# Pair 0 takes the raw first layer, four pairs take the cosine by a quarter turn, and the order is written anew

## The chip, the cores and the metric

The kernel runs on one core of a Trainium2 chip. A core has five engines that each work through their own instructions in program order: PE (matrix multiply, with PEld for its weight loads), DVE (vector), ACT (activation functions), POOL (general), and SP, which here only issues transfers. Sixteen DMA engines move the data. The metric is the device time of one execution in microseconds (us). Before the change it is 197.97 us, the median of 5 runs from 197.55 to 199.03.

## The reference

Two steps in a row. The first is a gated recurrence for 4 batches, 8 heads, 768 tokens and 48 channels per head. Every channel has a complex gate whose magnitude is capped, and a state:

```
scale = minimum(mag, 0.999) / (mag + 1e-06)        # mag = |a_re + i a_im|
new_re = ar*S_re - ai*S_im ;  new_im = ar*S_im + ai*S_re
S_re, S_im = new_re + k v^T, new_im
y[t] = q[t] . S_re
```

The second is a feed-forward block on x, the 384 values per token that the heads give together:

```
xn = (x - mu) / sqrt(var + 1e-06) * g_ln
out = x + maximum(xn @ w_ch1, 0) @ w_ch2           # 384 -> 1536 -> 384
```

## The kernel before

The tokens are cut into 24 chunks of 128; two chunks make a pair, so there are 12 pairs, three per batch. For a pair P the steps are named `step.P...`, and for a chunk n `step.n`. Pair 0 alone does its gate steps in two halves of four heads (`.0.0` and `.0.1`).

The gates go in logarithm and phase. `ln` takes the logarithm of a_re, `iv` its reciprocal, `r` the quotient a_im/a_re, `r2` and `u` the logarithm of 1+r*r, `l` the capped log magnitude (two DVE instructions, L449 and L451), `th` the arctangent of r. PE sums both along the tokens by triangular matrices: `dec` (L459) and `ph` (L474, L477). `e` and `en` are the exponentials of the decay. The phase stands in PSUM as turns scaled so that the low 16 bits of the word are the fraction of a turn; these are read as int16, which wraps the angle. `sin` (L502) reads them directly. For the cosine, `abs` (L496 on ACT or L498 on DVE) writes the absolute value to SBUF and `cos` (L505) takes the sine of a quarter minus it. `car` hands the phase to the next pair.

`ke` and `qe` scale k and q, `ks` and `qs` multiply them by cosine and sine, `kT`, `qT` transpose on PE and `ksT`, `qsT` copy the result out; from pair 3 on many of these are DMA transposes that SP issues (L566). `am` is the score matrix, `atm` masks it, `gm` and `G` carry the state, `y` is the output of a chunk, `x` its copy to SBUF.

For the feed-forward part, `bn` takes mean and variance of x, `xtr` and `xT` transpose x, `mm1.P.g.part` is the first layer in three groups g of two parts (L684, twelve matmuls a group), `relu.P.g` follows, `mm2.n.g` is the second layer (L705, four matmuls a step), and `ot` (L719; or `oa` on ACT and `ot` on POOL) scales by 1/sqrt(var) from `rstd` (POOL, L670 and L672), adds x, and `st` stores. The mean is not taken from x. It is taken out of the weights once: `wgc` builds a matrix of g_ln/384, `wp.g` multiplies w1 by it on PE (L367), and `wc.g.e`, nine DVE instructions (L371), replace w1 by g_ln*w1 minus that product. All first layers, pair 0's too, need `wc`.

w1 and w2 come by two transfers that POOL issues (`wl.0`, L350, and `wl.1`, L352), which also cast them to bf16. Two `gate` steps (L347) hold them back: POOL copies one element of a tile that SP loads, and so waits until it has landed.

The order on every engine is written out by hand in one string, `PLAN`: each word is a step, its engine and its PSUM bank. An engine does its steps in exactly that order; a step that waits holds all that follow it on its engine. `warm` steps are matmuls on constants that only keep PE running. `tab` steps load ACT's function table: logarithm and exponential are in one set, sine and arctangent in another.

Of the kernel before, what the change touches and what calls it, by code (L numbers as in the profile page):

```python
# [26 lines left out]
         "ks": 3, "qs": 3, "ksT": 4, "qsT": 4, "atm": 3, "G": 4, "x": 10, "stats": 4,  # L27
# [6 lines left out]
GATES = (("k", 0, 1), ("aim", 1, 0))  # L34
# [17 lines left out]
warm.60:P4 warm.61:P4 ph.1.0:P2 k.1.1:S qe.0.1.0:V cos.0.1:A qs.0.1.0:V cos.0.0:A dec.0.0:P1 sin.0.0:A0
aim.3.0:S vf.1.1:S k.1.0:S abs.1.0:V2 car.1.0:V2 vf.1.0:S q.1.1:S ks.0.1.0:G pad.qs.1:G mask:G tab.log.1:A
en.0.0:A1 e.0.0:A1 qs.0.1.1:V ke.0.0.0:V qe.0.0.0:V ks.0.0.0:V ks.0.0.1:V warm.62:P5 warm.63:P5 warm.64:P5
warm.65:P5 warm.66:P5 warm.67:P5 warm.68:P5 warm.69:P5 warm.70:P5 warm.71:P5 warm.72:P5 warm.73:P5
warm.74:P5 warm.75:P5 warm.76:P5 warm.77:P5 warm.78:P5 warm.79:P5 warm.80:P5 warm.81:P5 warm.82:P5 kT.1:P4
k.2.0:S wl.0:G qs.0.0.1:V u.1.0:A ln.2.0:A qs.0.0.0:V dps.0:P5 k.2.1:S iv.2.0:A l.1.0:V kT.0:P6 qT.1:P7
tab.trig.1:A cos.1.0:A v.0:A ksT.0:V6 r.2.0:G ksT.1:V4 decc.0:V5 wgc:V qsT.1:V7 qT.0:P0 gm.0:P1 dec.1.0:P4
am.1:P6 th.2.0:A sin.1.0:A2 tab.log.2:A e.1.0:A4 r2.2.0:G u.2.0:A pad.qs.2:G qsT.0:V0 am.0:P2 G.0:V1
atm.1:V6 atm.0:V2 y.1:P0 y.0:P6 ln.3.0:A iv.3.0:A wp.2:P7 qe.1.0.0:G x.0:A6 l.2.0:V dec.2.0:P2 wl.1:G  # L60
en.1.0:A4 wp.0:P6 e.2.0:A2 x.1:A0 wc.2.0:V7 wc.2.2:V7 en.2.0:A2 are.4.0:S xtr.0:P0 wc.2.1:V7 dps.1:P7
xtr.1:P4 r.3.0:G xT.0:A0 wp.1:P5 decc.1:A7 ph.2.0:P2 wc.0.0:V6 wc.0.1:V6 bn.0:V wc.0.2:V6 r2.3.0:A xT.1:A4
wc.1.2:V5 wc.1.1:V5 wc.1.0:V5 ke.1.0.0:G ke.1.0.1:G ks.1.0.0:G v.1:G qe.1.0.1:G mm1.0.2.1:P6 gm.1:P1 G.1:V1
mm1.0.2.0:P6 relu.0.2:V6 u.3.0:A aim.4.0:S ks.1.0.1:V qs.1.0.1:V qs.1.0.0:V bn.1:V rstd.0:G abs.2.0:A2
tab.trig.2:A th.3.0:A cos.2.0:A mm1.0.0.1:P4 mm1.0.1.1:P0 mm1.0.0.0:P4 relu.0.0:V4 sin.2.0:A2 k.3.0:S
q.2.1:S mm1.0.1.0:P0 ph.3.0:P6 l.3.0:V relu.0.1:A0 kT.3:P2 gm.2:P3 vf.2.0:S q.2.0:S k.3.1:S kT.2:P0 qT.2:P1
ksT.2:V0 qsT.2:V1 mm2.0.0:P4 mm2.0.1:P4 mm2.0.2:P4 sin.3.0:A6 am.2:P0 abs.3.0:A6 G.2:A3 ksT.3:A2 ke.2.0.0:G
gm.3:P3 qT.3:P5 ke.2.0.1:V ks.2.0.0:V tab.log.3:A ln.4.0:A iv.4.0:A ks.2.0.1:G r.4.0:G atm.2:V0 mm2.1.0:P2
mm2.1.1:P2 qsT.3:V5 vf.2.1:S aim.6.0:S am.3:P0 mm2.1.2:P2 car.3.0:A6 G.3:V3 q.3.1:S q.4.1:S ot.0:V4 kT.5:P3
atm.3:V0 tab.trig.3:A th.4.0:A qe.2.0.1:G qe.2.0.0:G y.2:P5 q.3.0:S are.6.0:S vf.3.1:S st.0:S y.3:P4 x.2:A5  # L70
x.3:A4 kT.4:P6 xtr.2:P7 ot.1:V2 bn.2:V xT.2:V7 xtr.3:P2 xT.3:V2 ksT.4:V6 dec.3.0:P0 mm1.1.0.1:P4
mm1.1.0.0:P4 r2.4.0:A mm1.1.1.1:P6 qs.2.0.1:V qs.2.0.0:V qT.5:P2 mm1.1.1.0:P6 ksT.5:V3 bn.3:V qT.4:P3
tab.log.4:A en.3.0:A0 v.2:A e.3.0:A0 relu.1.1:A6 ph.4.0:P0 relu.1.0:V4 vf.3.0:S gm.4:P4 ke.3.0.1:G qsT.4:V3
am.4:P6 qsT.5:V2 mm2.2.0:P5 am.5:P2 mm2.2.1:P5 tab.trig.4:A cos.3.0:A G.4:A4 rstd.1:G ke.3.0.0:G qe.3.0.1:G
are.5.0:S aim.5.0:S abs.4.0:V0 sin.4.0:A0 car.4.0:A0 atm.4:V6 mm1.1.2.0:P6 dps.3:P4 mm1.1.2.1:P6 tab.log.5:A
u.4.0:A atm.5:V2 qe.3.0.0:G ks.3.0.1:G ks.3.0.0:V qs.3.0.1:V relu.1.2:V6 qs.3.0.0:V y.5:P0 y.4:P1 l.4.0:V
mm2.3.0:P2 x.5:A0 kT.7:P3 mm2.3.1:P2 x.4:A1 xtr.4:P0 mm2.2.2:P5 xtr.5:P1 ln.5.0:A k.4.0:S iv.5.0:A decc.3:A4
ln.6.0:A q.4.0:S k.5.1:S v.3:G ksT.7:V3 dec.4.0:P6 xT.5:V1 xT.4:A0 mm2.3.2:P2 e.4.0:A6 en.4.0:A6 iv.6.0:A
bn.4:V mm1.2.1.1:P0 ot.2:V5 r.5.0:G qsT.7:S r.6.0:G r2.5.0:V mm1.2.1.0:P0 gm.6:P3 qe.4.0.1:V bn.5:V rstd.2:G
ke.4.0.0:G relu.2.1:A0 u.5.0:A mm1.2.0.1:P4 mm1.2.0.0:P4 tab.trig.5:A th.5.0:A mm1.2.2.1:P6 qe.4.0.0:G  # L80
am.7:P0 mm1.2.2.0:P6 ot.3:V2 qsT.6:S ksT.6:S k.5.0:S vf.4.1:S th.6.0:A relu.2.2:A6 vf.4.0:S st.2:S cos.4.0:A
G.6:V3 k.4.1:S q.5.1:S st.1:S gm.7:P3 dps.4:P2 relu.2.0:V4 mm2.5.0:P4 atm.7:V0 l.5.0:V am.6:P0 atm.6:V0
are.8.0:S y.7:P5 mm2.5.1:P4 q.5.0:S ph.5.0:P6 aim.7.0:S mm2.4.0:P0 y.6:P1 x.7:A5 xtr.7:P5 mm2.5.2:P4
r2.6.0:V bn.7:V ke.4.0.1:G v.4:V x.6:V1 xtr.6:P1 sin.5.0:A6 abs.5.0:A6 xT.7:A5 cos.5.0:A decc.4:A2
mm2.4.1:P0 mm2.4.2:P0 are.7.0:S k.6.1:S G.7:V3 ot.5:V4 tab.log.6:A u.6.0:A xT.6:V1 qs.4.0.0:V mm1.3.0.0:P6
dec.5.0:P4 ks.4.0.1:V mm1.3.1.1:P2 ks.4.0.0:V gm.8:P1 mm1.3.0.1:P6 mm1.3.1.0:P2 qs.4.0.1:V ot.4:V0 e.5.0:A4
qe.5.0.0:G kT.9:P0 en.5.0:A4 relu.3.0:A6 kT.8:P4 st.4:S l.6.0:V ln.8.0:A ksT.8:A4 G.8:A1 bn.6:V st.3:S
k.6.0:S qsT.9:S relu.3.1:V2 qe.5.0.1:V qs.5.0.0:V rstd.3:G q.6.1:S aim.8.0:S st.5:S mm1.3.2.0:P6 qT.8:P5
mm1.3.2.1:P6 ln.7.0:A gm.9:P1 relu.3.2:A6 vf.5.0:S mm2.7.0:P4 dec.6.0:P2 qs.5.0.1:G qsT.8:V5 mm2.7.1:P4
iv.7.0:A G.9:V1 ksT.9:V0 ke.5.0.0:V en.6.0:A2 am.8:P6 e.6.0:A2 r.7.0:V vf.5.1:S ph.6.0:P0 mm2.7.2:P4  # L90
qT.10:P5 am.9:P2 vf.6.1:S r2.7.0:A iv.8.0:A ke.5.0.1:V atm.8:V6 ks.5.0.0:G ks.5.0.1:G u.7.0:A y.8:P6 x.8:A6
tab.trig.6:A sin.6.0:A0 r.8.0:G ke.6.0.0:G qT.11:P7 qsT.10:V5 atm.9:V2 qsT.11:V7 mm2.6.0:P5 mm2.6.1:P5
y.9:P6 abs.6.0:A0 car.6.0:A0 kT.10:P7 bn.8:V x.9:V6 ksT.10:V7 xtr.8:P2 kT.11:P3 xtr.9:P6 mm2.6.2:P5 xT.9:A6
xT.8:V2 ksT.11:V3 am.10:P0 vf.6.0:S th.7.0:A mm1.4.1.0:P6 am.11:P2 th.8.0:A ke.6.0.1:G v.5:G mm1.4.1.1:P6
ot.6:V5 oa.7:A4 k.8.1:S are.9.0:S mm1.4.0.0:P4 mm1.4.0.1:P4 atm.10:V0 gm.10:P0 relu.4.1:A6 l.7.0:V
ks.6.0.1:V ph.7.0:P6 y.10:P1 cos.6.0:A atm.11:V2 G.10:V0 y.11:P0 relu.4.0:A4 mm2.9.0:P2 mm1.4.2.1:P4 x.10:V1
x.11:V0 r2.8.0:A mm1.4.2.0:P4 mm2.8.0:P3 dec.7.0:P0 mm2.8.1:P3 mm2.9.1:P2 ks.6.0.0:G car.7.0:A6 sin.7.0:A6
tab.log.7:A ln.9.0:A q.6.0:S q.8.0:S bn.9:V bn.10:V abs.7.0:A6 e.7.0:A0 qe.6.0.1:G qe.6.0.0:G rstd.4:G
ot.7:G v.6:G relu.4.2:V4 mm2.8.2:P3 xtr.10:P4 bn.11:V qs.6.0.0:V en.7.0:A0 qs.6.0.1:V gm.12:P5 dps.6:P6
# [102 lines left out]
def kernel(  # L202
# [54 lines left out]
    def T(name, i):  # L257
        return tiles[name][i % RINGS[name]]
# [512 lines left out]
```

## Time and profile before

| what | value |
|---|---|
| median of 5 runs | 197.97 us |
| the profiled execution's own time | 198.91 us |
| its span, first to last instruction | 197.0 us |
| PE busy | 176.4 us, of which `warm` (L734) 11.1 |
| DVE / ACT / POOL busy | 160.1 / 164.0 / 107.9 us |
| data moved | 37.76 MB, mean 192 GB/s |

The page shows the busy time of each engine, a strip of the span in 40 slices (digits are tenths busy; the line of the PE clock is what was granted), the DMA queues, the chain of work that ended last, and the costliest groups of instructions. A group's line gives the engine, the operation, output and inputs, the shapes, the count, the busy time with the mean of one in ns, and the idle time of the engine before these instructions with what ended it. Other views list instructions in order of time, or the busy time in chosen stretches.

### The profile page before, as it was taken

Reading aid. Unit: us, or ns where it says so; the run is one execution under the profiler, and the core shown is the slowest. Engines: PE = TensorE matmul, PEld = TensorE weight load, DVE = VectorE, ACT = ScalarE, POOL = GpSimd, SP = SyncE. Lnnn points to the kernel's source line nnn. Section 1 sums busy time; section 2 is a strip of 40 time slices with the busy share of each in tenths; the row PEclk is TensorE's granted clock in tenths of the full one; section 3 lists DMA queues with packets and bytes.
Section 4 is the critical chain, followed back from the end, with each engine's and each line's share of the span. In section 5 each row is a group of like instructions: output and inputs, shape, how many; then the busy total and the mean of one; then the engine's idle time right before and its main releaser. Section 6 shows DMA issues by size and latency. Waiting matters only on the chain.

```text
span 197.0 us, 5115 instructions
## 1 busy us (share of the span) xinstructions
PE 176.4 (90%) x2032; PEld 134.7 (68%) x2032; DVE 160.1 (81%) x268; ACT 164.0 (83%) x226; POOL 107.9 (55%) x127
## 2 busy tenths in 40 slices
PE   4788467989999999899999997999999999997992
PEld 3575443576787777587887785787877768686771
DVE  1359999899999999999998799699969969835702
ACT  4799994999899999999999999997979999464260
POOL 8545558435939268134958699325981376430230
PEclk9999965899999999999999999999999999999999
DMA  5999998999899599899899999999998999994222
GB/s 138 230 235 251 178 238 113 189 218 235 174 254 223 113 173 244 211 242 247 162 206 224 221 147 281 181 209 236 234 199 149 154 212 136 235 194 137 80 83 82
DMA packets 132937, 37.76 MB, mean 192 GB/s; under 512 B 127921, under 2 KB 132529, under 8 KB 132913
## 3 DMA queue, kind: packets, MB, share of 16 engines
q1 hardware_dynamic: 130960, 35.07, 85.6%
q0 software_dynamic: 1952, 2.36, 7.4%
q8 instruction: 16, 0.26, 0.5%
q14 instruction: 9, 0.07, 0.1%
HBM read 28.31 MB, written 4.72 MB: 168 GB/s over the span
## 4 chain that ended last, share of the span: by engine, by line
PE 46%; DVE 22%; ACT 10%; DMA 9%; issue 5%; SPq 3%; POOL 2%; DVEq 0%; POOLq 0%; ACTq 0%
PE banks L705 16%; PE banks L684 13%; DMA qsT<-qs 5%; DVE atm L280 4%; PE banks L584 3%; SPq L566 3%; DVE l L449 3%; PE banks L459 3%; DVE l L451 2%; DVE h L697 2%; PE banks L561 2%; DMA are<-in_a_re_dram 2%; DMA q<-in_q_dram 2%; ACT L739 2%; DVE w1b L371 2%
## 5 line engine op out<-in xcount | busy, mean ns | idle before, releaser
L705 PE MATMUL banks<-w2b,h 128*128 128x384 bf16 x288 | 55.5, 326 | 1.2 <-DVE atm L280 1.1
L684 PE MATMUL banks<-xT,w1b 128*128 128x256 bf16 x432 | 52.4, 272 | 1.0 <-DVE w1b L371 0.5
L684 PEld LDWEIGHTS <-w1b 128*128 128x128 bf16 x432 | 41.3, 98 | 7.9 <-issue 2.0
L705 PEld LDWEIGHTS <-h 128*128 128x128 bf16 x288 | 26.2, 97 | 14.9 <-issue 1.6
L280 DVE TENSOR_TENSOR atm<-banks,mask 128x1024 bf16<-128x1024 f32 x24 | 28.8, 1216 | 4.3 <-PE banks L584 4.2
L695 ACT ACTIVATE h<-banks 128x1024 bf16<-128x1024 f32 x27 | 27.0, 1022 | 6.3 <-PE banks L684 6.2
L739 ACT ACT_TABLE_LOAD x20 | 25.7, 1283 | 1.1 <-PEq L755 0.8
L280 POOL TENSOR_TENSOR ks<-ke,trig 128x768 bf16<-128x768 bf16 (+1 forms) x11 | 17.9, 1635 | 12.0 <-DVE ke L280 7.4
L280 POOL TENSOR_TENSOR qe<-q,e 128x384 bf16<-128x384 f32 x16 | 15.8, 996 | 13.2 <-ACT e L463 9.7
L280 POOL TENSOR_TENSOR r<-aim,are 128x768 f16<-128x768 f32 (+1 forms) x9 | 16.7, 1851 | 10.8 <-ACT are L433 10.8
L280 POOL TENSOR_TENSOR ke<-k,en 128x384 bf16<-128x384 f32 x17 | 17.1, 1014 | 8.8 <-ACT en L463 8.1
L719 DVE SCALAR_TENSOR_TENSOR ot<-banks,rstd,x 128x384 f32<-128x384 f32 x20 | 12.0, 609 | 8.8 <-PE banks L705 6.0
L584 PE MATMUL banks<-qsT,ksT 128*128 128x128 bf16 x192 | 15.3, 227 | 2.9 <-DVE qsT L277 1.6
L584 PEld LDWEIGHTS <-ksT 128*128 128x128 bf16 x192 | 13.0, 102 | 5.3 <-issue 3.7
L734 PE MATMUL banks<-u_e 128*128 128x256 f16 x83 | 11.1, 296 | 2.8 <-POOL u_e L312 2.8
L449 DVE SCALAR_TENSOR_TENSOR l<-r,w 128x768 f16<-128x768 f16 (+1 forms) x13 | 12.8, 988 | 0.9 <-ACT r L445 0.8
L647 DVE BATCH_NORM_STATS2 stats<-x 128x6 f32<-128x384 bf16 x24 | 13.1, 548 | 0.3 <-ACT x L275 0.3
L459 PE MATMUL banks<-l,u_e 128*128 128x384 f16 (+1 forms) x52 | 10.6, 328 | 3.1 <-DVE l L451 2.6
L634 PE MATMUL banks<-v,atm 128*128 128x48 bf16 x192 | 12.2, 186 | 0.9 <-DVE atm L280 0.8
L280 DVE TENSOR_TENSOR qs<-qe,trig 128x768 bf16<-128x768 bf16 (+1 forms) x21 | 12.1, 596 | 1.1 <-POOL qe L280 0.8
L431 ACT ACTIVATE w<-are 128x768 f32<-128x768 f32 (+1 forms) x13 | 10.3, 793 | 3.1 <-DMA are<-in_a_re_dram 3.0
L634 PEld LDWEIGHTS <-atm 128*128 128x128 bf16 x192 | 10.9, 98 | 2.8 <-DVE atm L280 1.7
(91 smaller groups left out, 374.0 us busy)
## 6 DMA issues: line engine op xcount, KB each, us to landing
k<-in_k_dram SPq DMA_DIRECT2D x24, 192.0 KB, 4.1
q<-in_q_dram SPq DMA_DIRECT2D x24, 192.0 KB, 4.2
vf<-in_v_dram SPq DMA_DIRECT2D x24, 192.0 KB, 4.4
out_dram<-ot SPq DMA_DIRECT2D x24, 192.0 KB, 3.2
are<-in_a_re_dram SPq DMA_DIRECT2D x11, 384.0 KB, 4.7
aim<-in_a_im_dram SPq DMA_DIRECT2D x11, 384.0 KB, 5.3
w1b<-in_moe_w_ch_dram POOLq DMA_DIRECT2D x1, 1152.0 KB, 11.9
w2b<-in_moe_w_ch_dram POOLq DMA_DIRECT2D x1, 1152.0 KB, 11.6
```

Source lines behind the costliest of these rows:

```text
L280: {"DVE": nc.vector, "POOL": nc.gpsimd}[eng(name)].tensor_tensor(**kw)
L449: nc.vector.scalar_tensor_tensor(out=S_("l"), in0=S_("r2"), scalar=0.5, in1=S_("w"), op0=ALU.mult, op1=ALU.add)
L459: nc.tensor.matmul(heads(ps[:, c]), lhsT=u_e[:, c, j], rhs=step(T("l", P), j), start=(j == 0), stop=(j == R - 1))
L584: nc.tensor.matmul(ps[:, h], lhsT=T("ksT", n)[:, h], rhs=T("qsT", n)[:, h], start=True, stop=True)
L634: nc.tensor.matmul(ps[:, h], lhsT=T("atm", n)[:, h], rhs=T("v", P)[:, c, h], start=True, stop=nfirst)
L647: nc.vector.bn_stats(out=T("stats", n), in_=T("x", n))
L684: nc.tensor.matmul(ps[:, jj], lhsT=w1b[:, dc, ts(gi * JG + jj, C)], rhs=T("xT", P)[:, dc].rearrange("p c t -> p (c t)"), start=(dc == 0), ...
L695: act(out=dst, in_=src, func=AF.Relu)
L705: nc.tensor.matmul(bank(f"o.{n}")[:, 0:DM], lhsT=T("h", P)[:, j, ts(c, C)], rhs=w2b[:, j], start=(j == 0), stop=(j == NJ - 1))
L719: nc.vector.scalar_tensor_tensor(out=T("ot", n), in0=bank(f"o.{n}")[:, 0:DM], scalar=T("rstd", P)[:, ds(c, 1)], in1=T("x", n), op0=ALU.mul ...
L734: g.add(f"warm.{i}", lambda i=i: nc.tensor.matmul(bank(f"warm.{i}")[:, 0:256], lhsT=u_e[:, 0, 0], rhs=u_e[:, 1].rearrange("p j t -> p (j t ...
L739: g.add(f"tab.{nm}.{i}", lambda tab=tab: nc.scalar.preload_act_table_set(tab))
```

## The change

Three edits to the steps, one new order.

1. Pair 0 centres its own tokens. A new DVE step `xc.n` (n = 0, 1) subtracts the mean that `bn` found; `xtr` transposes `xc`; `xT` multiplies by g_ln while it copies, in three instructions instead of one. So `mm1.0` needs only the raw w1 (`wl.0`). `wp` and `wc`, which overwrite w1, now come behind the parts of `mm1.0`.
2. For pairs 0 to 3 `abs` goes. A new PE step `qt` adds a quarter turn to the phase in PSUM by one matmul per chunk, after `sin` and `car` have read it, and `cos` reads the int16 in PSUM as `sin` does.
3. `rstd` may run on ACT (a logarithm and an exponential of 128x2); `l` is split into two steps, `l` and `lc`; the `gate` steps go; all constants wait for `ue`, the first step on POOL.

`PLAN` is a new string throughout. Counted by step: `rstd` POOL 12 to 4, ACT 0 to 8; `ks` POOL 11 to 5, DVE 15 to 21; `ke` POOL 17 to 13, DVE 7 to 11; `qs` POOL 5 to 9, DVE 21 to 17; `ot` POOL 4 to 10 (with `oa` on ACT 4 to 10), DVE 20 to 14; `x` ACT 17 to 11, DVE 7 to 13; `relu` ACT 27 to 25, DVE 9 to 11; `car` ACT 7 to 3, DVE 2 to 6; `r` POOL 9 to 7, DVE 4 to 6; `abs` ACT 8 to 6, DVE 5 to 2; `tab` 20 to 21; `warm` 83 to 97; `ksT` by DMA 12 to 13, `xT` by DMA 2 to 3.

The core of the diff:

```diff
-GATES = (("k", 0, 1), ("aim", 1, 0))
+QUARTER = {0, 1, 2, 3}
+CENTRED = {0}
...
     g.add("wl.0", lambda: nc.gpsimd.dma_start(
-        out=w1b, in_=moe_w_ch1.rearrange("(dc p) j -> p dc j", p=C)), needs=["gate.0"])
+        out=w1b, in_=moe_w_ch1.rearrange("(dc p) j -> p dc j", p=C)))
...
-        g.add(o, wp, needs=["wgc", "wl.0"], ps=(o, 1))
+        g.add(o, wp, needs=["wgc", "wl.0"] + [f"mm1.{P}.{jb}.{part}" for P in CENTRED
+                                              for part in range(2)], ps=(o, 1))
...
+            if P in QUARTER:
+                def f_qt(X=X, view=view):
+                    ps = view(f"ph.{X}")
+                    for c in range(R):
+                        nc.tensor.matmul(ps[:, c], lhsT=pick[ds(HALF, 1)], rhs=qrow[ds(HALF, 1), 0:W],
+                                         start=False, stop=True, skip_group_check=True)
+                add(f"qt.{X}", f_qt, needs=[f"ph.{X}", f"sin.{X}", "qrow"]
+                    + ([] if last else [f"car.{X}"]), ps=(f"ph.{X}", nb))
+                add(f"cos.{X}", lambda fs=fs, v16=v16: act(
+                    out=T("trig", P)[:, 0, :, fs], in_=v16(), func=AF.Sin, scale=TWO_PI_SAFE / TURN),
+                    needs=[f"qt.{X}"], uses=[("trig", P)], ps=(f"ph.{X}", nb))
...
+            own = P in CENTRED
+            if own:
+                add(f"xc.{n}", lambda n=n, c=c: nc.vector.tensor_scalar(
+                    out=T("xc", n), in0=T("x", n), scalar1=T("mv", P)[:, c, 0:1], scalar2=None,
+                    op0=ALU.subtract), needs=[f"bn.{n}"], uses=[("x", n), ("mv", P), ("xc", n)])
+            xs = "xc" if own else "x"
...
+                if own:
+                    for dc in range(ND):
+                        if eng(f"xT.{n}") == "ACT":
+                            nc.scalar.mul(out=T("xT", P)[:, dc, c], in_=ps[:, dc],
+                                          mul=gln[:, ds(dc, 1)])
+                        else:
+                            nc.vector.tensor_scalar(
+                                out=T("xT", P)[:, dc, c], in0=ps[:, dc],
+                                scalar1=gln[:, ds(dc, 1)], scalar2=None, op0=ALU.mult)
...
+            if eng(f"rstd.{P}") == "ACT":
+                act(out=t, in_=T("mv", P)[:, :, 1], func=AF.Ln, bias=eps_b)
+                act(out=t, in_=t, func=AF.Exp, scale=-0.5)
+                return
```

The first POOL steps of the new order up to the two weight loads, and the PE steps around pair 0's first layer (other engines' steps left out):

```
POOL: ue mask pad.ks.2 pad.qs.2 car0.1 one zdec pad.ks.1 ident car0.0 pick pad.qs.1 r.0.1 qrow cmean
      pad.ks.0 pad.qs.0 qe.0.0.0 r.3.0 ke.1.0.0 qe.1.0.1 ke.1.0.1 wl.0 wl.1 qs.1.0.1 qe.2.0.1
PE:   y.0 y.1 gm.1 qt.3.0 kT.2 dec.2.0 qT.3 qT.2 gm.2 xtr.0 xtr.1 kT.3 gm.3 am.2 mm1.0.0.1 mm1.0.1.1
      mm1.0.0.0 mm1.0.2.1 mm1.0.2.0 y.2 wp.2 mm1.0.1.0 kT.4 wp.0 kT.5 dec.3.0 mm2.0.0 am.3 mm2.0.1
      wp.1 mm2.0.2 mm2.1.0 qT.4 y.3 mm2.1.1 mm2.1.2
```

In the order before, POOL reaches `wl.0` after `gate.0`, `ke.0.1.0`, `ks.0.1.0` and `mask`, and `wl.1` after four more, `r.2.0`, `r2.2.0`, `pad.qs.2` and `qe.1.0.0`; SP's first loads are the two halves of pair 0's a_re and a_im, where the new order begins with the whole a_re of pair 1. The ACT steps of the new order up to `iv.3.0` are: tab.log, ln.1, ln.0.0, iv.0.0, iv.1, ln.0.1, iv.0.1, tab.trig, th.0.0, th.0.1, tab.log, u.0.0, u.0.1, u.1, ln.2, iv.2, v.0, en.0.1, e.0.0, en.0.0, e.0.1, tab.trig, sin.0.0, th.1, sin.0.1, th.2, cos.0.0, cos.0.1, tab.log, ln.3, iv.3.

## The prediction

> **What bounds the kernel now.** I read the page's strip first, then long stretches of busy time, then the chain up to 60 us, then POOL's and SP's lists around the weight loads.
>
> ```profile
> PE   4788467989999999899999997999999999997992
> DVE  1359999899999999999998799699969969835702
> ACT  4799994999899999999999999997979999464260
> PEclk9999965899999999999999999999999999999999
> ```
>
> The four strips are one slice of 4.9 us per digit. PE is not full in the first nine slices and full almost always after; DVE and ACT are full from slice 4 to about 25 and then thin out. The clock falls in slices 6 to 8 only.
>
> ```profile
> 0.00:53.00 53.00, 39.96 (x393) 29.34 (x394) 41.67 (x68) 44.73 (x64) 31.07 (x51) 0.90 0.99 198
> 53.00:197.00 144.00, 136.44 (x1643) 105.39 (x1640) 118.46 (x201) 119.28 (x162) 76.87 (x77) 1.00 0.92 189
> ```
>
> Busy time of PE, PEld, DVE, ACT, POOL in two stretches, then clock, DMA share, GB/s. From 53 us PE has 136.4 of 144, and the last 3.7 us are the tail (last matmul at 193.3, then `ot` and a store). So behind 53 us at most about 4 us can be won, and what counts is how much PE work is done by then. 53.0 is the end of `mm2.1.2`, the last second-layer step of pair 0:
>
> ```profile
> 46.31 2.11 PE L705 MATMUL banks<-w2b,h 128*128 128x384 bf16 x12
> 52.18 0.81 PE L705 MATMUL banks<-w2b,h 128*128 128x384 bf16 x4
> ```
>
> The chain up to there is DVE nearly throughout; of 20 to 60 us:
>
> ```profile
> 22.26 1.86 DVE l L451
> 31.53 1.86 DVE l L451
> 33.43 1.44 PE banks L459 x4
> 36.26 1.41 DVE w1b L371 x2
> 38.27 2.26 DVE w1b L371 x4
> ```
>
> `l`'s second instruction takes 1.86 us twice, `wc` holds the chain for 3.7 us, and a `dec` takes 1.44 where later ones take 0.65. And the weight loads:
>
> ```profile
> 18.09 1.01 POOL L350 DMA_DIRECT2D w1b<-in_moe_w_ch_dram  x1
> 29.07 1.08 POOL L352 DMA_DIRECT2D w2b<-in_moe_w_ch_dram  x1
> ```
> ```profile
> 20.88 6.56 SPq L387 DMA_DIRECT2D k<-in_k_dram  x1
> 31.45 8.82 SPq L387 DMA_DIRECT2D k<-in_k_dram  x2
> ```
> ```profile
> w1b<-in_moe_w_ch_dram POOLq DMA_DIRECT2D x1, 1152.0 KB, 11.9
> w2b<-in_moe_w_ch_dram POOLq DMA_DIRECT2D x1, 1152.0 KB, 11.6
> ```
>
> w1 lands at 30.0, w2 at 40.7, 5.6 us before its first use at 46.3. While each moves, SP stands at single loads for 6.6 and 8.8 us.
>
> **The change, part by part.**
>
> *Totals by engine*, row means times step counts. PE: ten `qt` matmuls, six of 0.16 us and four of 0.08: +1.3; eleven transposes less at 0.056: -0.6. ACT: `abs` -1.3, shorter `cos` -0.6, `x` -6 x 0.48, `relu` -2 x 1.02, `car` -1.9, `r2` -1.7, against `oa` +6 x 0.59, one table +1.28, copies +3, and `rstd`: 16 tiny instructions between 0.16 us (the 48x8 copy) and 0.48 (the 128x384 copy), 2.6 to 7.7; I take 0.16, the nearer size. Sum 0 to +5, taken as +0.5. DVE: `ks` +6 x 0.67, `x` +6 x 0.55, `ke` +4 x 0.54, `relu` +2.4, `car` +2.3, `r` +1.9, `xc` and the three-piece `xT` +1.4, against `ot` -3.7, `abs` -2.5, `qs` -2.5, copies -3: about +6. POOL: -10. In the 144 us after 53, DVE and ACT have 25 us free each, so these totals alone cost nothing there; without that cover DVE's 6 us would be the price.
>
> *Table and order moves on ACT in the start.* By its own list the new order reaches `iv.3.0` after 21.5 us of instructions (means less 0.05 overlap). Its waits: first are tile, double the size of before's (that landed 2.7 us after issue, a median 384 KB load takes 4.7), so `ln.1` at about 4.8; `ln.0.0` for the third 192 KB, landed at 6.1 as in before; then `en.0.1` needs `l`, `lc` and `dec`, no wait left since ACT comes there at 16.9. So `iv.3.0` ends near 26.2. SP's list up to are.3 is 24 loads of 192 KB, 4.7 MB, at 0.2 MB/us landed by 22 to 24: no wait, little to spare.
>
> *The weight loads move back.* POOL is in order, so `r.3.0` waits for `iv.3.0` and holds all behind it: 26.2 + 2.0 (`r`) + 3 x 1.0 (`ke`, `qe`, `ke`) = 31.2 for `wl.0`, 13 us later than before's 18.1; `wl.1` 1.0 later. w1 lands at 31.2 + 11.9 = 43.1. w2 moves behind it. Lower end for its extra time: the page gives both transfers 7.4% of 16 engines' span, 14.6 us in all, so 31.2 + 14.6 = 45.8 if nothing else moved; but SP's queue is full. Upper end: another whole 11.6, 54.7. Between, before's w2 moved while the DMA was full from 32.0 to 40.7, 8.7 us: 51.8. I take 52.3, near that row, with half a us for what SP then adds.
>
> *Pair 0's first layer.* DVE's list up to `xc.0` is 28.35 us of work; before it DVE idles about 12 us (9.8 until `u.0.0` lets `l.0.0` start at 13.1, 1.5 for `cos.0.0`, small ones), so `xc.0` ends at 40.6, `xT.0` at 42.4, and `mm1.0.0.1` can start at 43.0, just as w1 lands. Before's began at 38.8. So the bypass of `wc` does not start pair 0 earlier: what it frees (nine `wc`, 6.2 us of DVE) the order spends on pairs 1 to 3. PE then needs 7.4 us for the steps listed up to `dec.3.0` (mm1 4.0, two `wp` 1.3, `dec` 0.65, `kT` and `y` 1.3, small waits): `mm2.0.0` could start at 50.4.
>
> *w2 is late.* It lands at 52.3, so PE stands 1.9 us at `mm2.0.0`; queued behind are `am.3` (DVE's `atm.3` waits for it), `wp.1` and both chunks' second layers. From there to the end of `mm2.1.2`: six mm2 steps 3.9, `am.3` 0.45, `wp.1` 0.66, `qT.4` 0.45, `y.3` 0.4 = 5.9, so 58.2.
>
> *Sum.* PE's work done by `mm2.1.2` is larger than before by `y.2`, `y.3` (0.8), three transposes (1.35) and `dec.3.0` (0.65) = 2.8, and 0.6 less follows: break-even is 53.0 + 3.4 = 56.4. So 58.2 - 56.4 = +1.8. On the profiled execution 198.91 + 1.8 = 200.7; that execution lies 0.94 above the median, so 199.8 as a median. With w2 at 51.8 or 54.7 it is +1.3 or +4.2.
>
> *The rest.* `rstd.11` brings a table load into the last layer: 1.28 + 0.3 on ACT beside 3.9 us of second layer, hidden; shown bare it would cost 1.6. One more transpose by DMA in each of `ksT` and `xT`: about 1.3 us of SP time each, beside full PE; if SP's queue ends last they cost up to 2.6. The longer `sin`-`qt`-`cos` path (0.33 us) lies under another ACT step between the two each time; bare, 5 x 0.33 = 1.6.
>
> *Rules against rows.* The row first: each weight load took 11.6 to 11.9 us. The Trainium skill, "DMA: Bandwidth & Descriptors", § Anatomy of one DMA, gives 2.0 us plus bytes over 436e3 per us; for 1.18 MB written that is an estimate of 4.7 us, so w2 would land well before 50.4 and the sum would be 50.4 + 5.9 - 56.4 = -0.1. The trace has more than twice that duration, so the row stands. On the other side, `l`'s second instruction took 0.36 us at 68 us and 1.86 while POOL worked at 22 and 31. The Trainium skill, "SBUF — State Buffer", § SBUF: two separate sides, says that DVE and GpSimd take a shared port by an exclusive lock; the row agrees, and 10 us less POOL work would then help DVE.
>
> **The rivals.**
>
> *Forecast, w2 late, some of it lost for good* (chance 0.45): 199 to 202.2.
>
> *The start pays* (0.30, faster). Before lost time in 26 to 36 us at half clock (`dec` 1.44 against 0.65, `wp` likewise: 0.8 + 3 x 0.2 or so each) and to the two 1.86 us `l` (3.0 together). The new order has `warm` and `qt` steps up to 31 us and no POOL work beside most of `l`. If 1.5 to 3 us of that returns and w2 lands before 50, `mm2.1.2` ends at 53.5 to 55: -1.5 to -3, 195 to 196.5. It decides by one thing: w2 landed before about 50.5. Against it: POOL's list ties both loads to `iv.3.0`.
>
> *Another wait later* (0.13). SP can move only some six loads from 31 to 52, so vf.2, k.3, q.3 land at 55 to 62 instead of before 58; or DVE, with 6 us more, lags where PE needs it in 60 to 120 us (it is 95% busy there). 3 to 5 us on top: 202.5 to 205.
>
> *No measurable change* (0.12): the late w2 is covered because PE comes late anyhow; 197 to 199.
>
> **How the numbers follow.** 0.5% (1 us) is about what a measurement of this kernel can tell. Faster takes 0.30; same 0.15, the fourth case and a little of the first; slower 0.55, the rest. Predicted 199.8, from the likeliest; alone its range is 199 to 202.2. For 8 in 10 the range goes from 195.6, most of the faster case, to 203.5, half of the third.
>
> **What would show it.** Right: `wl.0` issued at 30 to 33 us; PE idle just before the first L705 group, at 50 to 53 us, released by a DMA; `mm1.0` near 43; SP standing long at single loads from 32 to 52. Wrong: w2 landed before 50 us or `wl.0` before 28; the end of `mm2.1.2` before 56; or a large idle stretch of PE behind 60 us, which none of these sums holds.

## The result and the profile after

After: 199.86 us, the median of 26 executions (197.69 to 204.25). Before, on the same chips: 197.85 us, 47 executions (196.85 to 200.18). The ratio is 1.0069, with a 95% interval from 1.0049 to 1.0090, so the change made the kernel slower by about 0.7%. Executions over 1.5% above the fastest of their kernel are left out of every ratio here (six of after's 26, six of `w1_early`'s twelve, which took 203 to 207 us, and at most two of any other), so a ratio can differ from that of the medians beside it. The profiled execution took 199.70 us, with a span of 198.0 (before: 198.91 and 197.0).

The strips of the page, one digit per slice of 4.95 us:

```profile
PE   5567879887999999799989999999999999979992
DVE  0364989978798998999999999998887779967052
PEclk9999999999999999999999999999999999999998
```

Slices count from 0. The full clock is now there in every slice but the last. DVE is at 9 from slice 16 to 26 without a break. Behind slice 9, PE's thin places are 16 (7), 20 (8) and 35 (7), where before had 16 (8), 24 (7) and 36 (7): slices 16 and 20 begin at 79 and 99 us. The strip alone doesn't say which kernel loses more. The busy time in two stretches, cut at the end of `mm2.1.2` (PE, PEld, DVE, ACT, POOL, then clock, DMA share, GB/s):

```profile
0.00:55.10 55.10, 42.82 (x475) 32.22 (x476) 39.62 (x83) 49.99 (x71) 27.71 (x49) 1.00 1.02 211
55.10:198.00 142.90, 133.95 (x1573) 102.12 (x1571) 119.54 (x199) 115.32 (x166) 67.26 (x61) 1.00 0.88 185
```

`mm2.1.2` ends at 55.1 us, and 134.0 us of PE's work remain; before, it ended at 53.0 with 136.4 left. It ends 2.1 us later with 2.5 us less to do: measured by work left, the start is 0.4 us better than before's. The loss is behind it: PE idles 5.45 us between 55.1 and the last matmul at 194.5 (139.4 - 133.95), where before idled 3.86 (140.3 - 136.44). That is +1.6, and the tail behind the last matmul is 0.2 shorter: -0.4 + 1.6 - 0.2 = +1.0, the difference of the spans.

POOL's list around the weight loads, SP's list beside them, the time from issue to landing, and PE's first uses:

```profile
24.96 1.82 POOL L286 TENSOR_TENSOR r<-aim,are 128x768 f16<-128x768 f32 x1 [7.29 <-ACT are L443]
29.33 1.00 POOL L356 DMA_DIRECT2D w1b<-in_moe_w_ch_dram  x1
30.34 1.06 POOL L358 DMA_DIRECT2D w2b<-in_moe_w_ch_dram  x1
```
```profile
32.02 12.22 SPq L397 DMA_DIRECT2D vf<-in_v_dram  x2
44.33 6.43 SPq L397 DMA_DIRECT2D k<-in_k_dram  x3
```
```profile
w1b<-in_moe_w_ch_dram POOLq DMA_DIRECT2D x1, 1152.0 KB, 11.1
w2b<-in_moe_w_ch_dram POOLq DMA_DIRECT2D x1, 1152.0 KB, 18.8
```
```profile
40.48 3.45 PE L731 MATMUL banks<-xT,w1b 128*128 128x256 bf16 x30 [1.07 <-DMA w1b<-in_moe_w_ch_dram]
49.15 0.82 PE L753 MATMUL banks<-w2b,h 128*128 128x384 bf16 x4 [1.33 <-DMA w2b<-in_moe_w_ch_dram]
...
53.70 1.46 PE L753 MATMUL banks<-w2b,h 128*128 128x384 bf16 x8
```

(The end of 53.70 + 1.46 is that of `mm2.1.2`.) Both loads hang on `r.3.0`, which waits 7.3 us for ACT, as forecast. w1 lands at 40.4 and PE stands 1.07 us for it; w2 lands at 49.1, with 18.8 us instead of 11.6 from issue to landing, and PE stands 1.33 us. SP is held for 12.2 and 6.4 us by the loads that it issues meanwhile.

Where the later loss lies, by stretches that hold about the same work (before's are 2 us earlier):

```profile
73.00:108.00 35.00, 34.12 (x426) 26.56 (x424) 34.13 (x57) 34.29 (x47) 21.71 (x21) 1.00 0.96 217
108.00:163.00 55.00, 53.86 (x656) 41.28 (x654) 47.28 (x81) 49.63 (x69) 34.40 (x34) 1.00 1.07 202
```
```profile
75.00:110.00 35.00, 31.75 (x380) 23.73 (x378) 33.77 (x53) 30.55 (x42) 21.02 (x18) 1.00 0.94 198
110.00:165.00 55.00, 54.29 (x653) 41.28 (x651) 47.77 (x81) 52.79 (x78) 30.10 (x25) 1.00 0.96 200
```

From 75 to 110 us PE has 31.75 of 35, against 34.12 before: 2.4 us lost in one stretch. DVE is full there in both kernels. The next stretch is as good as before's.

### The profile page after: what moved, and what is told of

Its sections match the earlier page's. It is cut to its first block, busy times and chain, and to the rows that moved or that the text cites. A ratio compares the mean times of both kernels' runs of the same rounds, so it can differ in the third digit from the quotient of the medians.

```text
span 198.0 us, 5150 instructions
## 1 busy us (share of the span) xinstructions
PE 176.8 (89%) x2045; PEld 134.3 (68%) x2045; DVE 159.2 (80%) x281; ACT 165.3 (83%) x237; POOL 95.0 (48%) x109
## 4 chain that ended last, share of the span: by engine, by line
PE 32%; ACT 22%; DMA 18%; DVE 14%; issue 5%; SPq 4%; POOL 3%; DVEq 0%; ACTq 0%; POOLq 0%
PE banks L753 12%; DMA w2b<-in_moe_w_ch_dram 9%; PE banks L731 9%; ACT L787 5%; DMA are<-in_a_re_dram 4%; DMA out_dram<-ot 4%; SPq L591 3%; PE banks L609 3%; DVE l L459 3%; ACT w L441 2%; ACT h L743 2%; ACT r L455 2%; DVE l L462 2%; ACT e L474 2%; ACT are L443 1%
## 5 line engine op out<-in xcount | busy, mean ns | idle before, releaser
L753 PE MATMUL banks<-w2b,h 128*128 128x384 bf16 x288 | 54.0, 326 | 2.0 <-DMA w2b<-in_moe_w_ch_dram 1.3
L753 PEld LDWEIGHTS <-h 128*128 128x128 bf16 x288 | 26.5, 98 | 16.9 <-DMA w2b<-in_moe_w_ch_dram 1.7
L743 ACT ACTIVATE h<-banks 128x1024 bf16<-128x1024 f32 x25 | 25.0, 1027 | 7.6 <-PE banks L731 7.6
L286 POOL TENSOR_TENSOR r<-aim,are 128x768 f16<-128x768 f32 (+1 forms) x7 | 12.0, 1719 | 22.6 <-ACT are L443 22.6
L765 POOL TENSOR_TENSOR ot<-ot,x 128x384 f32<-128x384 f32 x10 | 9.6, 970 | 21.6 <-ACT ot L758 21.6
L745 DVE TENSOR_SCALAR h<-banks 128x1024 bf16<-128x1024 f32 x11 | 13.3, 1217 | 7.9 <-PE banks L731 7.9
L286 POOL TENSOR_TENSOR qs<-qe,trig 128x768 bf16<-128x768 bf16 x9 | 15.5, 1737 | 5.7 <-DVE qe L286 5.4
L286 POOL TENSOR_TENSOR ke<-k,en 128x384 bf16<-128x384 f32 x13 | 12.1, 939 | 9.3 <-ACT en L474 5.5
L782 PE MATMUL banks<-u_e 128*128 128x256 f16 x97 | 13.3, 296 | 2.2 <-POOL u_e L320 2.2
L489 PE MATMUL banks<-th,u_th 128*128 128x384 f16 (+1 forms) x52 | 11.9, 313 | 2.3 <-ACT th L478 2.3
L782 PEld LDWEIGHTS <-u_e 128*128 128x128 f16 x97 | 10.1, 106 | 4.1 <-POOL u_e L320 1.9
## 6 DMA issues: line engine op xcount, KB each, us to landing
w1b<-in_moe_w_ch_dram POOLq DMA_DIRECT2D x1, 1152.0 KB, 11.1
w2b<-in_moe_w_ch_dram POOLq DMA_DIRECT2D x1, 1152.0 KB, 18.8
```

The lines of the kernel that those rows point to most:

```text
L286: {"DVE": nc.vector, "POOL": nc.gpsimd}[eng(name)].tensor_tensor(**kw)
L489: nc.tensor.matmul(heads(ps[:, c]), lhsT=u_th[:, c, j], rhs=step(T("th", P), j), start=False, stop=(j == R - 1), skip_group_check=True)
L743: act(out=dst, in_=src, func=AF.Relu)
L745: nc.vector.tensor_scalar(out=dst, in0=src, scalar1=0.0, scalar2=None, op0=ALU.max)
L753: nc.tensor.matmul(bank(f"o.{n}")[:, 0:DM], lhsT=T("h", P)[:, j, ts(c, C)], rhs=w2b[:, j], start=(j == 0), stop=(j == NJ - 1))
L782: g.add(f"warm.{i}", lambda i=i: nc.tensor.matmul(bank(f"warm.{i}")[:, 0:256], lhsT=u_e[:, 0, 0], rhs=u_e[:, 1].rearrange("p j t -> p (j t ...
```

## The experiments

The theory of the forecast was the late w2. After the result there were others: the tail, where stores stand ahead of transposes in SP's list; the order of DVE between 75 and 110 us; and `rstd` on ACT. All kernels are after with one edit, except two that are before with one part of the change. An edit of `PLAN` is shown by the words beside the moved step. Ratios are to the kernel before, so after itself stands at 1.0069.

**The weight loads.** Earlier w1, and both loads later:

```diff
-... qe.0.0.0:G r2.2.0:V ... x.0:A2 wl.0:G tab.log.3:A ... wl.1:G qs.1.0.1:G
+... qe.0.0.0:G wl.0:G r2.2.0:V ... x.0:A2 tab.log.3:A ... wl.1:G qs.1.0.1:G    # w1_early
+... qe.0.0.0:G r2.2.0:V ... x.0:A2 tab.log.3:A ... qs.1.0.1:G wl.0:G wl.1:G    # w_later
```

> The changed kernel with one step moved: POOL issues the first weight load (wl.0) right after qe.0.0.0 instead of behind r.3.0, ke.1.0.0, qe.1.0.1 and ke.1.0.1, so at about 17 us instead of 29.3; w2 keeps its place at about 29 us. Theory A (the late weights cost the time, as predicted): PE's two waits of 1.07 us (w1) and 1.33 us (w2) go, and what they cost stays saved, 199.4 - 2.4 = 197.0, a ratio to the kernel before of 0.995 to 0.997. Theory B (the waits behind 75 us cost it): PE starts earlier but later waits for DVE take it back, less than 0.6 us, ratio 1.004 to 1.007. Theory C (loads that SP has queued behind w1 now come late): slower than the changed kernel, ratio above 1.009, with a DMA wait between 20 and 40 us.

> The changed kernel with both weight loads put behind qs.1.0.1 on POOL, about 6 us later (35 instead of 29.3 us). Theory A: each us that w2 is later is a us lost, +5 to +6 us, ratio about 1.035. Theory B: PE stands longer at mm1.0 and mm2.0, but DVE and ACT go on, and part is caught up before 75 us: +1 to +3 us, ratio 1.012 to 1.022.

`w1_early`: ratio 0.9997 (0.9968 to 1.0025). `wl.0` went at 17.4 us and `wl.1` at 31.0; w2 landed at 43.5, both waits were gone, and `mm2.1.2` ended at 53.4 instead of 55.1. The 1.7 us came through as about 1.4 (0.7% of 197.85). `w_later`: 1.0318 (1.0276 to 1.0360), some 5 us slower than after for loads issued 6 us later (35.3 and 36.3). Its longest wait (in total, times, longest):

```profile
PE banks L729 <- DMA w1b<-in_moe_w_ch_dram: 5.9, 1, 5.9
```

Not all of that is the wait. PE's granted clock was 0.59 from 45.2 to 51.1 us there, behind the wait, where after has 1.00, and the first part of pair 0's first layer took 5.79 us instead of 3.45. So a late weight costs, but this run's 5 us are not the price of the waiting alone: up to 2.3 of them go with the clock. In after the waiting at pair 0 is 2.4 us, and that is paid for by the better start.

**DVE's order and SP's order.** One step earlier for each named wait:

```diff
-... ks.4.0.1:V lc.5.0:V aim.7.0:S ... mm2.4.1:P1 dec.5.0:P4 ... th.8.0:A ks.6.0.1:V ... ot.7:G relu.4.1:V4 ...
+... ks.4.0.1:V aim.7.0:S ... mm2.4.1:P1 lc.5.0:V dec.5.0:P4 ... th.8.0:A relu.4.1:V4 ks.6.0.1:V ... ot.7:G ...   # dve_order
-... ot.15:V2 ks.11.0.0:V ... xT.20:V7 st.15:S ot.16:G ...
+... ot.15:V2 st.15:S ks.11.0.0:V ... xT.20:V7 ot.16:G ...                                    # store_early
```

> The changed kernel with two steps moved on DVE: lc.5.0 behind the masks of chunks 7 and 6 (before dec.5.0), and relu.4.1 ahead of ks.6.0.1. In the changed kernel's trace PE waits 1.11 us for the mask at 81 us and 0.97 us for that relu at 104 us. Theory A: these waits are paid anyhow by DVE, which is full there; no change, ratio 1.005 to 1.009. Theory B: both waits go, -1 to -2 us, ratio 0.997 to 1.002.

> The changed kernel with the store of chunk 15 issued by SP right after its ot step, ahead of the last eight transposes, instead of behind them. In the changed kernel's trace ACT waits 3.36 us at 175 us in oa.18, for the store that frees its buffer; st.18 and the two transposes of the last x stand behind it. Theory A and B: PE is kept busy by other work or by the last qsT, no change, ratio 1.005 to 1.009. Theory D (the tail costs it): -1 us or more, ratio below 1.003.

`dve_order`: 197.53 us, 0.9992 (0.9970 to 1.0014), a gain of some 1.5 us on after, though w2 was as late as in after (PE's wait for it 1.4). `store_early`: 202.92 us, 1.0273 (1.0235 to 1.0311), 4 us slower. The store, issued early, stands ahead of the last transposes:

```profile
PE banks L607 <- DMA qsT<-qs: 4.2, 2, 3.4
PE banks L729 <- ACT r L449: 1.8, 1, 1.8
```

The late store in after is the lesser evil, and behind the last matmul after is 0.2 us shorter than before: the tail is not where the loss is.

**`rstd` on POOL.** The eight `rstd` that the change put on ACT go back to POOL; then those of pairs 0 to 3 alone, the others alone, and, against it, the ACT instructions of pairs 0 to 3 issued twice:

```diff
-... rstd.0:A ... rstd.1:A ... rstd.2:A ... rstd.3:A ... rstd.5:A ... rstd.6:A ... rstd.7:A ... tab.log.10:A rstd.11:A
+... rstd.0:G ... rstd.1:G ... rstd.2:G ... rstd.3:G ... rstd.5:G ... rstd.6:G ... rstd.7:G ... rstd.11:G               # rstd_pool
+... rstd.0:G ... rstd.1:G ... rstd.2:G ... rstd.3:G ... rstd.5:A ... rstd.6:A ... rstd.7:A ... tab.log.10:A rstd.11:A  # rstd_first
+... rstd.0:A ... rstd.1:A ... rstd.2:A ... rstd.3:A ... rstd.5:G ... rstd.6:G ... rstd.7:G ... rstd.11:G               # rstd_last
```
```diff
                 act(out=t, in_=t, func=AF.Exp, scale=-0.5)
+                if P < 4:                                            # rstd_double
+                    act(out=t, in_=T("mv", P)[:, :, 1], func=AF.Ln, bias=eps_b)
+                    act(out=t, in_=t, func=AF.Exp, scale=-0.5)
                 return
```

> The changed kernel with all rstd steps on POOL again and without the last table load. In the changed kernel's trace a pair's rstd on ACT is 0.30 + 0.20 us, 8 pairs 4 us in all. Theory A and B: ACT has room, no change, ratio 1.005 to 1.009. Rival E (ACT in 55 to 75 and 110 to 140 us is the bound): -1 to -2 us, ratio below 1.002.

> After's order with rstd of pairs 0 to 3 alone on POOL; 5, 6, 7 and 11 and the last table load stay on ACT as in after (199.9). Theory (what costs is the full stretch from 55 to 110 us, where ACT, DVE and PE run in step): nearly all of the 4.9 us that all eight gave come back, 195.3 to 196.8. Rival (the later pairs, or the table load in the last layer): at most 1 us, 198.9 to 200.

> The complement: rstd of pairs 5, 6, 7 and 11 on POOL, the last table load gone, pairs 0 to 3 on ACT. Theory: 199 to 200, since ACT and DVE have slack behind 110 us and the table load lies beside the last second layers. Rival (tail and table load): 195.3 to 197.

> After with both ACT instructions of rstd issued twice for pairs 0 to 3, eight tiny instructions or 2.0 us more on ACT. Theory A (ACT's in-order time in that stretch is what PE ends up waiting for): 1.5 to 3 us slower than after, 201.4 to 203. Theory B (what costs is that the POOL work is moved and meets DVE, ACT's own time is covered): within 0.5 us of after, 199.4 to 200.4.

`rstd_pool`: 195.03 us, 0.9870 (0.9825 to 0.9915). `rstd_first`: 194.67 us, 0.9856 (0.9810 to 0.9901): four steps on another engine are worth the whole 2%, and this version beats both kernels. `rstd_last`: 197.85 us, 1.0037 (1.0009 to 1.0066): the later pairs and the table load in the last layer are worth some 0.3%, and the interval overlaps with after's. `rstd_double`: 198.66 us, 1.0046 (1.0016 to 1.0075): 2 us more work on ACT cost nothing, and in after's trace ACT does not stand idle before any of these four `rstd`. So the first theory, ACT's time in a full stretch, falls: what counts is not what `rstd` takes on ACT, but what it does on POOL.

DVE and POOL in after around 76 us, in order of time:

```profile
75.25 1.23 DVE L745 TENSOR_SCALAR h<-banks 128x1024 bf16<-128x1024 f32 x1 [0.38 <-PE banks L731]
76.39 1.18 DVE L286 TENSOR_TENSOR ke<-k,en 128x384 bf16<-128x384 f32 x1
77.68 0.56 DVE L286 TENSOR_TENSOR ks<-ke,trig 128x768 bf16<-128x768 bf16 x1
78.16 1.80 DVE L462 TENSOR_SCALAR l<-l 128x768 f16<-128x768 f16 x1
79.88 1.21 DVE L286 TENSOR_TENSOR atm<-banks,mask 128x1024 bf16<-128x1024 f32 x1
```
```profile
76.34 0.83 POOL L407 TENSOR_SCALAR v<-vf 128x768 bf16<-128x768 f32 x1
77.75 1.99 POOL L286 TENSOR_TENSOR ks<-ke,trig 128x768 bf16<-128x768 bf16 x1 [0.58 <-DVE ke L286]
```

and in `rstd_first`, with the same order on DVE:

```profile
74.51 1.23 DVE L743 TENSOR_SCALAR h<-banks 128x1024 bf16<-128x1024 f32 x1 [0.23 <-PE banks L729]
75.65 0.55 DVE L284 TENSOR_TENSOR ke<-k,en 128x384 bf16<-128x384 f32 x1
76.30 0.56 DVE L284 TENSOR_TENSOR ks<-ke,trig 128x768 bf16<-128x768 bf16 x1
76.78 0.35 DVE L460 TENSOR_SCALAR l<-l 128x768 f16<-128x768 f16 x1
77.05 2.35 DVE L284 TENSOR_TENSOR atm<-banks,mask 128x1024 bf16<-128x1024 f32 x2
```
```profile
75.86 0.41 POOL L715 TENSOR_SCALAR rstd<-mv 128x2 f32<-128x2 f32 x1
76.35 1.07 POOL L717 TENSOR_TENSOR rstd<-rstd,half_n 128x2 f32<-128x2 f32 x1
77.41 0.83 POOL L405 TENSOR_SCALAR v<-vf 128x768 bf16<-128x768 f32 x1
78.20 1.63 POOL L284 TENSOR_TENSOR ks<-ke,trig 128x768 bf16<-128x768 bf16 x1
```

In after, DVE's `ke` starts 0.05 us after POOL's `v` and takes 1.18 us instead of 0.55; `lc` (L462) starts inside POOL's `ks` and takes 1.80 instead of 0.35, ending where `ks` ends. From the start of the `relu` (L745) to that of the score mask `atm`, 4.63 us pass. In `rstd_first` POOL is busy with its two tiny `rstd` instructions at that moment, `v` and `ks` come behind DVE's short steps, and the same way takes 2.54 us. The Trainium skill, "SBUF — State Buffer", § SBUF: two separate sides, describes this as an exclusive lock that whoever starts first holds for the whole instruction, for DVE instructions in a two-port mode or, against a POOL instruction that reads SBUF, with two SBUF inputs. The trace agrees: `lc` ends 0.2 us after `ks` does (79.96 against 79.74), whatever its own 0.35.

What DVE loses there reaches PE. In after PE stands for that mask, and later for a `relu`:

```profile
81.15 0.20 PE L659 MATMUL banks<-v,atm 128*128 128x48 bf16 x1 [1.11 <-DVE atm L286]
104.39 1.47 PE L731 MATMUL banks<-xT,w1b 128*128 128x256 bf16 x12 [0.97 <-DVE h L745]
```

`rstd_first` has neither wait. From the end of `mm2.1.2` to the last matmul PE idles 5.45 us in after and 2.4 in `rstd_first`. The same holds across the runs: in all seven kernels that have pair 2's `rstd` on ACT and `lc` of pair 5 in after's place (after, `w1_early`, `w_later`, `store_early`, `quarter_undone`, `rstd_last`, `rstd_double`), this `lc` takes 1.79 or 1.80 us and PE then waits 1.06 to 1.30 for the mask; in `rstd_pool` and `rstd_first` it takes 0.35, and PE does not wait.

This can be counted over the stretch from 58 to 110 us, where all these kernels do the same 17 DVE instructions of four kinds. The sum of their groups `l`, `lc`, `ks` and `ke`, worked out from the groups by shape, beside PE's busy time from 75 to 110 us:

| kernel | ratio | the four groups, us | PE busy of 35 us |
|---|---|---|---|
| after | 1.0069 | 4.5 + 2.9 + 4.1 + 2.3 = 13.8 | 31.75 |
| rstd_last | 1.0037 | 5.1 + 2.9 + 4.2 + 2.3 = 14.5 | 31.75 |
| rstd_double | 1.0046 | 4.6 + 3.4 + 4.1 + 2.3 = 14.4 | 31.79 |
| quarter_undone | 1.0086 | 4.9 + 3.4 + 3.8 + 1.8 = 13.9 | 32.78 |
| w1_early | 0.9997 | 5.2 + 3.4 + 4.6 + 1.9 = 15.1 | 31.99 |
| dve_order | 0.9992 | 3.8 + 2.1 + 3.4 + 2.3 = 11.6 | 32.70 |
| rstd_pool | 0.9870 | 3.8 + 1.6 + 3.3 + 1.6 = 10.3 | 34.45 |
| rstd_first | 0.9856 | 3.8 + 1.6 + 3.3 + 1.6 = 10.3 | 34.45 |

At their shortest (0.95, 0.35, 0.55 and 0.55 us) the 17 would take 10.2. After pays 3.6 us above that, `rstd_first` almost none. The sum separates the two kernels with the short `lc` from the others; among the others it does not order the times. The two groups that moved most, in after and in `rstd_first`:

```profile
L462 DVE TENSOR_SCALAR l<-l 128x768 f16<-128x768 f16 x4 | 2.9, 716 | 0.1
L286 DVE TENSOR_TENSOR ke<-k,en 128x384 bf16<-128x384 f32 x3 | 2.3, 759 | 0.0
```
```profile
L460 DVE TENSOR_SCALAR l<-l 128x768 f16<-128x768 f16 x4 | 1.6, 406 | 0.1
L284 DVE TENSOR_TENSOR ke<-k,en 128x384 bf16<-128x384 f32 x3 | 1.6, 549 | 0.0
```

`dve_order` is a second, independent way out of the same meeting: it moves that very `lc` (of pair 5) behind `atm`, where it took 0.35 us, and gets part of the gain (it moves a `relu` too, so their shares are not separated). `w1_early` has the most of these meetings and gains all the same, at pair 0. What was not tried is to move pair 2's `rstd` alone, or to hold back `v` and `ks` alone with `rstd` left on ACT. That ACT's time is not the cause is shown, and that the place of the first four `rstd` on POOL is; that `v` and `ks` at 76 us are the whole of it is read from the traces.

**Both ways together.** `rstd_pool` with the two DVE moves:

> All rstd on POOL and the two DVE moves (lc.5.0 ahead of dec.5.0, relu.4.1 ahead of ks.6.0.1). If the two losses are separate, their gains add: 195.0 - 2.4 = 192.6 (192.2 to 193.4). If both are the same lag of DVE between 75 and 110 us, the second adds little: 194.4 to 195.3.

197.77 us, 1.0020 (0.9992 to 1.0049): neither theory's number, 1.5% slower than `rstd_pool` alone. The moved `lc` and the next pair's `l` now meet POOL's `ks` and `ke`, and the moved `relu` waits for PE:

```profile
79.10 1.02 DVE L460 TENSOR_SCALAR l<-l 128x768 f16<-128x768 f16 x1
83.30 1.67 DVE L457 SCALAR_TENSOR_TENSOR l<-r,w 128x768 f16<-128x768 f16 x1
100.11 1.22 DVE L743 TENSOR_SCALAR h<-banks 128x1024 bf16<-128x1024 f32 x1 [1.65 <-PE banks L729]
```

The first two are `lc` and `l` of pairs 5 and 6 (0.35 and 0.95 in `rstd_pool`), the third is a `relu` that stands 1.65 us for its first layer, with DVE's whole list behind it (in `rstd_pool` it did not wait). Each edit is good in the other's absence: what these edits change is which instructions meet.

**The parts of the change in the order before.** The quarter turn alone, and the centring of pair 0 alone, both with before's order and its `gate` steps, and otherwise after's code. In the first, `abs` is taken out and `qt` put in behind `sin` and `car`; in the second, `xc` comes in behind `bn`, and `wp` and `wc` go behind pair 0's second layer:

```diff
-QUARTER = set()
+QUARTER = {0, 1, 2, 3}          # quarter_alone
-CENTRED = set()
+CENTRED = {0}                   # centre_alone
```

> The kernel before with its own order, and the quarter turn for pairs 0 to 3 alone: five abs gone, ten short matmuls added, sin ahead of qt ahead of cos, car.3 and cos.3 moved up beside it; one small constant more on POOL. Theory A: the start before is bound by DVE, which loses 1.5 us of work by 18 us, so -0.5 to -1.5 us, ratio 0.992 to 0.998. Rival: the path sin, qt, cos is longer by a PE step each time and cos.1 now ends later on ACT, 0 to +1 us, ratio 1.0 to 1.005.

> The kernel before with its own order, and pair 0's own centring alone: bn and xc for both chunks behind l.2 on DVE, x.1 right behind x.0 on ACT, wp and wc behind pair 0's second layer instead of ahead of its first. w1 lands at 30 us there, so pair 0's first layer can start at about 36 us instead of 38.8. Theory A: nine wc (6.2 us of DVE) leave the path to the first layer, and come back between 52 and 62 us where DVE is as full: 0 to -1.5 us, ratio 0.993 to 1.0. Rival: they delay the masks of pair 1 there and pair 1's first layer waits for them, +1 to +3 us, ratio 1.005 to 1.015.

Both were slower than either of their theories had it. `quarter_alone`: 199.35 us, 1.0089 (1.0051 to 1.0127). `centre_alone`: 204.80 us, 1.0359 (1.0332 to 1.0386), where PE stands for the weights being centred and for `l`:

```profile
PE banks L589 <- DVE w1b L384: 3.0, 1, 3.0
PE banks L473 <- DVE l L465: 2.4, 1, 2.4
```

The nine `wc` are only moved from one full place of DVE's list to another. And the quarter turn undone in after's order (`abs` back on ACT or DVE, `cos` from its result):

```diff
-QUARTER = {0, 1, 2, 3}
+QUARTER = set()
-... qt.0.0:P0 ... qt.0.1:P3 ... cos.0.0:A0 cos.0.1:A3 ...
+... abs.0.0:A0 ... abs.0.1:V3 ... cos.0.0:A cos.0.1:A ...
```

> The changed kernel without the quarter turn: abs and the old cosine stand where qt and the new one stood (abs on ACT for half 0.0 and pairs 2 and 3, on DVE for half 0.1 and pair 1). By the rows this gives 2.1 us back to ACT and 1.5 us to DVE, all before 38 us, and takes ten short matmuls from PE. Theory A: the start is bound by the weight transfers at 40 and 49 us, so up to 2 us of this are hidden; the ratio rises from 1.007 to 1.01 at most. Rival: the start is bound by ACT (its chain up to iv.3.0 sets the weight loads, and half of the work removed lies ahead of it), +2 us, ratio 1.015 to 1.02.

199.94 us, 1.0086 (1.0048 to 1.0125): no difference from after that these runs can tell. In its profiled execution `mm2.1.2` ends 1.2 us later than in after, and PE is busy 1.0 us more from 75 to 110 us. So neither part gains by itself in before's order, and undoing the quarter turn changes nothing measurable in after's. No run has the new order without the parts, so what the order is worth alone is not shown.

## Why the prediction was right or wrong

The number was right: 199.8 forecast, 199.86 measured, slower. The reasons were half right, and that the two agree so closely is luck, as the end of this section shows.

- *POOL holds both loads behind `iv.3.0`.* Right in kind. `iv.3.0` ended at 24.9 (26.2 forecast) and `wl.0` went at 29.3 (31.2).
- *w2 lands at 52.3, bounds 51.8 to 54.7, lower end 45.8.* It landed at 49.1, between the lower end and the bounds. Counted from the issue of `wl.0`, it took 19.8 us, where 21.1 was taken; of the miss of 3.2 us, 1.9 is the earlier issue. The estimate from the Trainium skill, "DMA: Bandwidth & Descriptors", § Anatomy of one DMA, 4.7 us per load, falls short by a factor of 2.4 (11.1 us) and 4 (18.8 us).
- *`mm1.0` at 43.0, just as w1 lands.* It started at 40.5, with 1.07 us of waiting for w1 that the sum did not have; w1 was the late one first. `xc` was ready by 37.5 instead of 40.6. The second instruction of `l`, twice 1.85 us in before's start, took 0.35 there; how much of the 3 us that is was not separated. PE's granted clock from 20 to 40 us, 0.74 in before, is 1.00 here, which the sum did not have and the rival that the start pays did.
- *PE stands 1.9 us at `mm2.0.0`; `mm2.1.2` ends at 58.2, break-even 56.4.* It stood 1.33 and ended at 55.1. The break-even was too late as well: with 2.5 us less work left than before, not 3.4, it lies at 55.5. So the sum's term of +1.8 measured as -0.4. **This is the step that failed.** The rival that the start pays named the decider, w2 before 50.5, and 53.5 to 55 for the end; that much of it came true.
- *Nothing is lost later, because ACT, DVE and POOL have slack in total.* Wrong: 2.4 us were lost from 75 to 110 us. DVE was full there, and what its instructions take depends on POOL. The total was even right in the wrong way: DVE's busy time was to grow by 6 us and fell by 0.9, as its instructions were slowed less: added up over the traces, they lie 16.9 us above the shortest of their shape in before and 11.0 in after. In the first 55 us that is 6.1 and 1.3 (3.0 of it the two `lc` of the start), but from 55 to 110 us 4.5 in before, 5.4 in after and 2.2 in `rstd_first`. Against before it is less the amount that changed there than its place, just ahead of a mask that PE waits for.
- *`rstd`'s 16 instructions at 0.16 us, 2.6 in all, hidden.* They took 0.30 and 0.20, 4.0 in all, and were hidden, as the doubling of the first four shows. The cost was in what the forecast did not price at all, the place that they left empty on POOL; as the traces read, it brought `v` and `ks` forward onto DVE's `ke` and `lc`. The rule on the lock was cited, with the sign that less POOL work helps DVE. It helped in the start; at 76 us the moved POOL work did harm.
- *The table load of `rstd.11` is hidden.* `rstd_last` bounds it, with three other `rstd`, at a few tenths of a per cent.
- *The rival of a later wait (0.13), DVE lagging from 60 to 120 us.* Its place and its engine were right, its 3 to 5 us on top of a late w2 were not: 1.6 us, net, on a start that gained.

- *Readings of the views.* Two were loose, and the sum does not rest on them: ACT's strip has a 4 between its full slices (it is busy 1.9 of the 5 us from 30 us), and the 8.8 us of SP are two loads, not one.

So errors of opposite sign met: the start was 2.2 us better than forecast, what follows 1.6 worse and the tail 0.2 better, which makes +1.0 of span where +1.8 was forecast. The rest of the agreement is the choice of executions: before's profiled one lay 0.94 us above the median that was known, after's 0.16 below its own. By the ratio, the change costs 1.4 us, or 199.2 from before's 197.85.

## What to carry to other kernels

Where DVE is the full engine, price a step that leaves POOL as well as one that comes to it: look up which DVE instructions stand beside POOL's next two steps, and compare the long and the short duration of the same shape in the trace. Slack in totals says nothing about a stretch where two engines hold each other up, and gains from two moves there need not add. A transfer's time from issue to landing is to be taken from a moment with the same load on the other queues, not from its median.

## What the hardware showed unexpectedly

- Four pairs of tiny instructions more on POOL (0.9 to 1.5 us each) made the kernel 2.1% faster (0.9856 against 1.0069), as the traces read, by the steps that they held back.
- The same fp16 `lc` of 128x768 took 0.35 us alone and 1.80 beside POOL's `ks`; `ke` of 128x384 took 0.55 and 1.18.
- POOL is slowed in the same meetings: in `rstd_first` its `rstd` instructions took 0.41 and 1.07 us beside DVE's short steps at 76 us, and 0.22 and 0.70 at 93.
- One weight load of 1152 KB took 9.6 to 19.1 us from issue to landing over these runs, the longest where both were under way together; while both move in after, SP is held 12.2 us at two loads.
- PE's granted clock is 1.00 from 20 to 40 us in after, where before's strip falls to 6, 5 and 8; after has 19 `warm` matmuls and its `qt` there, before neither. `quarter_undone`, with 17 `warm` and no `qt`, stays at full clock; `quarter_alone`, with `qt` and no `warm` there, falls to 5 and 5. So the `qt` is not what does it; the `warm` steps alone were not tried.
